# Half-height products from unit 16 on, and weight casts moved to casting transfers, in a convolution with two gated layers

## The chip, the cores and the metric

The kernel runs on one core of a Trainium2 chip. The metric is the device time of one execution in microseconds; the median of three runs of the kernel before is 1130.21 us (1130.08 to 1131.05).

## The reference

Three stages on 2 x 4096 tokens with 192 channels, all in float32:

```python
w = softmax(weight)                       # 8 heads x 7 taps
x = sum over k of w[h, k] * x_pad[s + k]  # causal convolution, 24 channels to a head
h = x @ w_in                              # 192 -> 2048
g = where(h >= 1, h, where(h <= -1, 0, (h + 1)**2 / 4))
x = g @ w_out                             # 2048 -> 192
h = x @ w_in2
out = (h * sigmoid(1.702 * h)) @ w_out2
```

## The kernel before, in words

**Tiles.** The tokens are cut into 16 tiles of 512 (channels on partitions). A layer's 2048 hidden channels are cut into 16 blocks `f` of 128. A *phase* is (layer, token tile); there are 32, and each has 16 *units*, one to a block: 512 units in the order `units`. Units 0 to 31 alternate between the two first phases, four or so at a time (phase 0 has units 0-3, 8-11, 16-19 and 22-25; phase 1 has 4-7, 12-15, 20-21 and 26-31); phase 2 begins with unit 32 and phase 3 with unit 40.

**Precision.** Every float32 operand is split in a high part that TensorE's fp32r format holds and a low part, the difference. A product is hi x hi + hi x lo + lo x hi. 192 channels are 128 + 64 rows: the 64 rows of the high part and the 64 of the low part stand together in a tile `xb`, and swapped (low above) in a tile `xc`, which two SP transfers make from `xb` (`swap_halves`, L184).

**Two forms of the products.** `gemm1` and `gemm2` (L250, L309) work a unit with five products of 128 rows each. `both` (L341) works a *couple*: gemm1 of units u and u + 1 and gemm2 of u - 4 and u - 3, as 38 products of 64 rows in 19 pairs, one in the lower and one in the upper half of the array. In it a unit's gemm1 has nine pieces, because the product lo x lo of the last 64 rows is left out; gemm2 has ten. An even unit reads `xb`, an odd one `xc`. The lower halves of unit u come in pairs 0 to 4, those of unit u + 1 from pair 5 on (its third kind, `xc`, in pair 8), the upper halves of both behind the upper halves of gemm2.

**Two loops.** Up to step `WHOLE` (L511) a step is gemm1 of unit `step`, gemm2 of unit `step - 4`, the activation of the unit (`act_a`: ScalarE twice, then VectorE's max-min L283; `act_b`: ScalarE's cast and VectorE's subtraction, L74 and L75), then what `plan` holds for the step (`beside`). From `WHOLE` on (L525) an iteration is a couple, then `act_a` of both units, `act_b` of both, `beside` of both steps, and last `finish`, which turns a finished phase into the next layer's x tile or into output. The first iteration of this loop still uses gemm1 and gemm2. The order of the program is the order of every engine's queue (`manual_schedule`, L451).

**Weights.** Each tile (layer n, block f) comes as 64-bit words by SP (`weight_load`, L97) and is made into fp32r parts in four pieces (`weight_ops`, L102): begin (ScalarE L118, VectorE's shift L119), join (VectorE L123), high part (a cast, L129, on ScalarE or VectorE), low part (two VectorE subtractions, L133 and L134). `convert_at` (L488) puts these into four consecutive steps from `s` on. For layer 1, f = 8 to 15, `s` is 7, 8, 10, 12, 13, 15, 17, 18; for layer 2, f = 0 to 7, it is 22, 23, 25, 26, 28, 29, 30, 31.

**The start.** SP loads taps, x tiles and the first weight tiles; TensorE does the convolution of a part of the first tiles with diagonal matrices (`conv_on_pe`, L167); the order from L475 on is written by hand. `put_b` (L188) writes `xb` of a layer-1 tile and swaps it only where its phase starts at or behind `WHOLE`. The load of tile (1, 3) is issued by L481, behind that list.

Of the kernel before, what the change touches and what calls it, by code (L numbers as in the profile page):

```python
# [8 lines left out]
F32 = mybir.dt.float32  # L9
F32R = mybir.dt.float32r  # L10
U32 = mybir.dt.uint32
# [4 lines left out]
P = 128  # L16
T = 512
# [3 lines left out]
def kernel(  # L21
# [21 lines left out]
    nc = tc.nc  # L43
    NBLK, D, _ = out.shape
    K = taps_in.shape[2]
    NF, _, WC = w1.shape
    DB = D - P
    B = P // DB
# [1 line left out]
    H = P // 2  # L50
    LAG = 4
    CH = 4
    WHOLE = 2 * NF
    BY_DVE = {(1, f) for f in range(CH, NF, 3)} | {(2, 0), (2, 3)}

    const = ctx.enter_context(tc.tile_pool(name="const", bufs=1))
    wpool = ctx.enter_context(tc.tile_pool(name="wpool", bufs=1))
    stage = ctx.enter_context(tc.tile_pool(name="stage", bufs=2))
# [2 lines left out]
    xs_p = ctx.enter_context(tc.tile_pool(name="xs", bufs=4))  # L61
    a_p = ctx.enter_context(tc.tile_pool(name="a", bufs=3))
    g_p = ctx.enter_context(tc.tile_pool(name="g", bufs=LAG))
    o_p = ctx.enter_context(tc.tile_pool(name="o", bufs=2))
    ps = ctx.enter_context(tc.tile_pool(name="ps", bufs=1, space=bass.MemoryType.PSUM))

    def bank(n, name):
        return ps.tile([P, T], F32, tag=f"bank{n}", name=name)

    def f32(ap):  # L70
        return ap.bitcast(F32)

    def split(src, hi, lo):
        nc.scalar.copy(hi, src)  # L74
        nc.vector.tensor_sub(lo, src, f32(hi))  # L75


    taps = const.tile([P, 2, K], F32, name="taps")
    ident = const.tile([P, P], F32, name="ident")
# [22 lines left out]
    def weight_ops(n, f, s):  # L102

        low, high = s[:, :, 0], s[:, :, 1]  # L110
        w = wt[n][:, f, :]
        m = WC - DB
        st = {}

        def begin():
            a = stage.tile([P, WC], F32, tag="wa", name="wa")
            d = stage.tile([P, WC], U32, tag="wd", name="wd", bufs=3)
            nc.scalar.activation(a, f32(high), AF.Prelu, scale=2.0**-112, alpha=-(2.0**32))  # L118
            nc.vector.tensor_single_scalar(d, low, 29, op=ALU.logical_shift_right)  # L119
            st["a"], st["d"] = a, d  # L120

        def join():
            nc.vector.scalar_tensor_tensor(  # L123
                st["d"], st["a"].bitcast(U32), 3, st["d"], op0=ALU.logical_shift_left, op1=ALU.bitwise_or
            )

        def high_part():
            cast = nc.vector.tensor_copy if (n, f) in BY_DVE else nc.scalar.copy
            cast(w[:, 0:WC], f32(st["d"]))  # L129

        def low_part():
            d = f32(st["d"])
            nc.vector.tensor_sub(w[:, WC + DB : 2 * WC], d[:, 0:m], f32(w[:, 0:m]))  # L133
            nc.vector.tensor_sub(w[:, WC : WC + DB], d[:, m:WC], f32(w[:, m:WC]))  # L134

        return [begin, join, high_part, low_part]


    x1, x2 = {}, {}

    def new_xs():
        return [xs_p.tile([P, T], F32R, tag=t, name=t) for t in ("xah", "xal", "xb", "xc")]
# [21 lines left out]
        for k in range(2):  # L164
            nc.tensor.matmul(w.rearrange("p (k c) -> p k c", c=P), ones, wide, start=k == 0, stop=False)  # L165

    def conv_on_pe(part, t, c, ident, eng_mul, n, fresh):  # L167

        d = o_p.tile([P, K, P], F32, tag="o", name="diag")
        for k in range(n):  # L170
            eng_mul(d[:, k], ident, taps[:, part, k : k + 1])

        def tap(k):
            return lambda: nc.tensor.matmul(c, d[:, k], t[:, k : k + T], start=fresh and k == 0, stop=k == n - 1)  # L174

        return [tap(k) for k in range(n)]

# [6 lines left out]
    def swap_halves(dst, src):  # L184
        nc.sync.dma_start(f32(dst[0:DB]), f32(src[DB:P]))
        nc.sync.dma_start(f32(dst[DB:P]), f32(src[0:DB]))

    def put_b(i, c):  # L188

        b, halved = i % B, phases.index((1, i)) * NF >= WHOLE  # L190
        t = x1[i][2 + (b if halved else 0)]
        hi, lo = (t[0:DB], t[DB:P]) if b == 0 else (t[DB:P], t[0:DB])
        split(c[b * DB : (b + 1) * DB], hi, lo)
        if halved:
            swap_halves(x1[i][3 - b], t)

    def conv_ops(j):

# [19 lines left out]
    phases = [(1, 0), (1, 1), (2, 0), (2, 1), (1, 2)]  # L218
# [4 lines left out]
    def in_turn(*runs):  # L223
        made, us = {}, []
        for p, n in runs:
            f = made.get(p, 0)
            us += [(p, f + k) for k in range(n)]
            made[p] = f + n
        return us

    units = in_turn((0, 4), (1, 4), (0, 4), (1, 4), (0, 4), (1, 2), (0, 4), (1, 6))
# [10 lines left out]
    def hidden_w(u):  # L242
        n, f = phases[units[u][0]][0], units[u][1]
        return wt[n][:, f, 0 : 2 * P], wt[n][:, f, WC + DB : WC + DB + 2 * P]

    def x_of(u):
        n, i = phases[units[u][0]]
        return (x1 if n == 1 else x2)[i]

    def gemm1(u):  # L250

        ah, al, b, _ = x_of(u)
        h = hid[u] = bank(HID + u % 4, f"h{u}")
        hi, lo = hidden_w(u)
        a = [(hi[:, 0:P], ah), (lo[:, 0:P], ah), (hi[:, 0:P], al)]
        bs = [(lo[:, P : 2 * P], b), (hi[:, P : 2 * P], b)]
        prods = a[0::2] + a[1:2] + bs if u < CH else a[0:2] + bs + a[2:]
        for j, (w, r) in enumerate(prods):
            nc.tensor.matmul(h, w, r, start=j == 0, stop=j == len(prods) - 1)  # L259
# [118 lines left out]
    def finish(p, step):  # L378
        n, i = phases[p]
        acc_a, acc_b = accs.pop(p)  # L380
        if n == 1:
            ah, al, b, c = x2[i] = new_xs()
            s = cv_p.tile([P, T], F32, tag="cva", name="s")
            nc.scalar.copy(s[0:DB], acc_b[DB:P])

            def add():
                nc.vector.tensor_add(s[0:DB], acc_b[0:DB], s[0:DB])  # L387

            def put():
                split(s[0:DB], b[0:DB], b[DB:P])  # L390
                if phases.index((2, i)) * NF >= WHOLE:
                    swap_halves(c, b)

            if i < B:
                add()
                split(acc_a, ah, al)
                put()
            else:
                split(acc_a, ah, al)
                at(step + 1, add)  # L400
                at(step + 2, put)
        else:
            o = o_p.tile([P, 2, T], F32, tag="o", name="o")
            nc.scalar.copy(o[0:DB, 1], acc_b[DB:P])
            nc.vector.tensor_add(o[0:DB, 1], acc_b[0:DB], o[0:DB, 1])
            if p < len(phases) - 1:
                nc.scalar.copy(o[:, 0], acc_a)
                nc.sync.dma_start(out[i, 0:P], o[:, 0])
                nc.sync.dma_start(out[i, P:D], o[0:DB, 1])
            else:  # L410
                near, far = slice(0, T // 2), slice(T // 2, T)
                nc.scalar.copy(o[:, 0, near], acc_a[:, near])  # L412
                nc.sync.dma_start(out[i, 0:P, near], o[:, 0, near])
                nc.scalar.copy(o[:, 0, far], acc_a[:, far])  # L414
                nc.scalar.dma_start(out[i, 0:P, far], o[:, 0, far])
                nc.sync.dma_start(out[i, P:D], o[0:DB, 1])


    plan, xt, raw = {}, {}, {}

    def at(step, op):
        plan.setdefault(max(step, 0), []).append(op)
# [4 lines left out]
    def weights_at(n, f):  # L427
        ops = []

        def piece():  # L430
            if (n, f) in raw:
                ops.extend(weight_ops(n, f, raw.pop((n, f))))
            ops.pop(0)()

        return [piece] * 4

    def fetch_x(*which):
        for part, i in which:
# [12 lines left out]
    with tc.manual_schedule():  # L451
# [7 lines left out]
        cb_ps, ca_ps = bank(3, "cb_ps"), bank(2, "ca_ps")  # L459
# [6 lines left out]
            x1[i] = new_xs()  # L466
        ca = cv_p.tile([P, T], F32, tag="cva", name="cva")
        a0 = conv_taps(0, xt[0, 0], ca)
        b_ops = conv_on_pe(1, xt[1, 0], cb_ps, ident, nc.scalar.mul, K, True)
        a1 = conv_on_pe(0, xt[0, 1], ca_ps, ident, nc.gpsimd.tensor_scalar_mul, K - 1, False)  # L470
        for op in b_ops:
            op()

# [14 lines left out]
        def convert_at(n, f, steps):  # L488
            at(steps[0] - 3, lambda: fetch_w(n, f))
            for step, op in zip(steps, weights_at(n, f)):  # L490
                at(step, op)

        for f in range(CH, NF):
            s = f - 2 if f < 2 * CH else 2 * CH - 1 + 5 * (f - 2 * CH) // 3
            convert_at(1, f, range(s, s + 4))
        for f in range(NF):
            s = (22, 23, 25, 26, 28, 29, 30, 31)[f] if f < NF // 2 else 36 + (3 * f - 3 * NF // 2) // 2
            convert_at(2, f, range(s, s + 4))
        for j in range(1, NBLK // B):
            conv_at(j)  # L500

# [8 lines left out]

        for step in range(WHOLE):  # L511
            gemm1(step)
# [6 lines left out]
            if step >= LAG:  # L519
                act_b(step - 1)  # L520
            if step == WHOLE - 1:
                act_b(step)
            beside(step)

        for u in range(WHOLE, len(units) + LAG + 4, 2):  # L525
            v = u - LAG
            if u == WHOLE:
                gemm1(u)
# [70 lines left out]
```

## Time and profile before

| | |
|---|---|
| median of 3 runs | 1130.21 us |
| profiled execution | 1130.99 us, span 1129.2 us |
| TensorE products (PE) | 1124.0 us busy, 9452 |
| TensorE weight loads (PEld) | 921.2 us |
| VectorE (DVE) | 716.0 us, 63% |
| ScalarE (ACT) | 821.2 us, 73% |
| GpSimd (POOL) | 5.9 us, all of it at the start |
| granted clock of TensorE | 1.00 |
| stores of `o`, issue to landing | 2.0 us (256 KB), 2.3 us (128 KB) |

Busy shares are means over the whole span. ScalarE and VectorE are much busier in the first 90 us, in which the weights are made, than later. Idle time of an engine other than the one that ends the chain costs nothing by itself.

### The profile page before, as it was taken

The page shows a single profiled execution, that of the slowest core. Times are in us where ns is not written, and L with a number is a line of the kernel's source. Part 1 is how long each engine was busy: PE and PEld are TensorE (multiplying, and loading weights), DVE is VectorE, ACT ScalarE, POOL GpSimd, SP SyncE. Part 2 cuts the span into 40 slices and gives each one's busy share as a digit, 9 for nine tenths or more (in the row PEclk, how much of TensorE's full clock was granted, in tenths as well). Part 3 has the DMA queues.
Part 4 walks back from the last instruction along what each step waited for, and adds up shares of the span by engine and source line. Part 5 has one row for each costly group of instructions (what it writes and reads, how often), then busy time and mean ns, then how long its engine had stood idle before and what let it go on. Part 6 is the DMA issues. An engine that isn't in the chain of part 4 may idle for free.

```text
span 1129.2 us, 23095 instructions
## 1 busy us (share of the span) xinstructions
PE 1124.0 (100%) x9452; PEld 921.2 (82%) x9452; DVE 716.0 (63%) x1159; ACT 821.2 (73%) x1463; POOL 5.9 (1%) x12
## 2 busy tenths in 40 slices
PE   9999999999999999999999999999999999999998
PEld 5888888888888888888888888888888888888886
DVE  7998867765647656475664756657565575655532
ACT  7998678867768677676876758677586776868654
POOL 2000000000000000000000000000000000000000
PEclk9999999999999999999999999999999999999999
DMA  5434111000010000100010000100001000000000
GB/s 161 140 117 148 34 40 37 11 20 15 11 39 15 20 15 19 40 6 20 15 47 16 2 20 15 49 15 1 20 15 48 16 1 20 15 20 15 11 15 15
DMA packets 16840, 36.68 MB, mean 32 GB/s; under 512 B 2528, under 2 KB 2784, under 8 KB 16736
## 3 DMA queue, kind: packets, MB, share of 16 engines
q1 hardware_dynamic: 16592, 35.09, 10.8%
q8 instruction: 74, 1.21, 0.5%
q14 instruction: 30, 0.25, 0.1%
q10 hardware_dynamic: 144, 0.13, 0.0%
HBM read 21.05 MB, written 6.29 MB: 24 GB/s over the span
## 4 chain that ended last, share of the span: by engine, by line
PE 100%; issue 0%; ACT 0%; DVE 0%
PE acc L370 48%; PE h L370 43%; PE h L259 3%; PE acc L324 3%; PE cb_ps L174 1%; PE ca_ps L174 0%; PE ca_ps L165 0%; ACT o L414 0%; DVE ones L162 0%; ACT o L412 0%
## 5 line engine op out<-in xcount | busy, mean ns | idle before, releaser
L370 PE MATMUL acc<-ghi,wt 64*128 64x512 f32 x2868 | 869.6, 386 | 0.0
L370 PE MATMUL h<-xah,wt 64*128 64x512 f32 x1912 | 738.2, 386 | 0.0
L370 PE MATMUL acc<-glo,wt 64*128 64x512 f32 x1912 | 705.3, 386 | 0.0
L370 PEld LDWEIGHTS acc<-ghi,wt 64*128 64x128 f32 x2868 | 489.5, 184 | 56.3
L75 DVE TENSOR_TENSOR glo<-a,ghi 128x512 fp32r<-128x512 f32 x512 | 341.5, 688 | 231.5 <-ACT ghi L74 221.3
L370 PEld LDWEIGHTS h<-xah,wt 64*128 64x128 f32 x1912 | 351.8, 184 | 37.8 <-issue 0.4
L370 PEld LDWEIGHTS acc<-glo,wt 64*128 64x128 f32 x1912 | 351.8, 184 | 37.8 <-DVE glo L75 0.2
L370 PE MATMUL h<-xal,wt 64*128 64x512 f32 x956 | 369.1, 386 | 0.0
L74 ACT CAST ghi<-a 128x512 fp32r<-128x512 f32 x512 | 301.8, 615 | 28.7 <-DVE a L283 28.5
L283 DVE SCALAR_TENSOR_TENSOR a<-h,a 128x512 f32<-128x512 f32 x256 | 176.6, 690 | 157.6 <-ACT a L282 157.3
L285 ACT ACTIVATE a<-h 128x512 f32<-128x512 f32 x256 | 150.3, 595 | 147.7 <-PE h L370 136.5
L370 PE MATMUL h<-xb,wt 64*128 64x512 f32 x717 | 238.7, 386 | 0.0
L370 PE MATMUL h<-xc,wt 64*128 64x512 f32 x717 | 238.7, 386 | 0.0
L281 ACT ACTIVATE a<-h 128x512 f32<-128x512 f32 x256 | 151.0, 590 | 55.2 <-PE h L370 53.3
L370 PEld LDWEIGHTS h<-xal,wt 64*128 64x128 f32 x956 | 175.9, 184 | 18.7
L282 ACT ACTIVATE a<-a 128x512 f32<-128x512 f32 x256 | 161.9, 632 | 8.2
L370 PEld LDWEIGHTS h<-xc,wt 64*128 64x128 f32 x717 | 131.9, 184 | 17.7
L370 PEld LDWEIGHTS h<-xb,wt 64*128 64x128 f32 x717 | 131.9, 184 | 10.5
L155 DVE SCALAR_TENSOR_TENSOR cva<-xt,taps,cva 128x512 f32<-128x512 f32 x90 | 67.4, 749 | 1.3
L155 DVE SCALAR_TENSOR_TENSOR cvb<-xt,taps,cvb 128x512 f32<-128x512 f32 x42 | 31.3, 746 | 0.5
L74 ACT CAST xb<-s 64x512 fp32r<-64x512 f32 x16 | 9.9, 621 | 29.2 <-DVE s L387 29.2
L324 PE MATMUL acc<-ghi,wt 128*128 128x512 f32 x102 | 29.0, 391 | 0.0
(64 smaller groups left out, 405.1 us busy)
## 6 DMA issues: line engine op xcount, KB each, us to landing
raw<-in_w_dram SPq DMA_DIRECT2D x32, 448.0 KB, 3.4
xc<-xb SPq DMA_DIRECT2D x46, 128.0 KB, 2.3
xt<-in_xa_dram SPq DMA_DIRECT2D x16, 259.0 KB, 2.9
out_dram<-o SPq DMA_DIRECT2D x15, 256.0 KB, 2.0
out_dram<-o SPq DMA_DIRECT2D x17, 128.0 KB, 2.3
xt<-in_xb_dram SPq DMA_DIRECT2D x8, 259.0 KB, 3.1
xb<-xc SPq DMA_DIRECT2D x14, 128.0 KB, 2.2
out_dram<-o ACTq DMA_DIRECT2D x1, 128.0 KB, 1.8
```

Of the source, the lines that this page charges most:

```text
L74: nc.scalar.copy(hi, src)
L75: nc.vector.tensor_sub(lo, src, f32(hi))
L155: return lambda: nc.vector.scalar_tensor_tensor(c, x, w, c, op0=ALU.mult, op1=ALU.add)
L174: return lambda: nc.tensor.matmul(c, d[:, k], t[:, k : k + T], start=fresh and k == 0, stop=k == n - 1)
L259: nc.tensor.matmul(h, w, r, start=j == 0, stop=j == len(prods) - 1)
L281: nc.scalar.activation(a, h, AF.Relu, bias=0.5, scale=0.5)
L282: nc.scalar.activation(a, a, AF.Square)
L283: nc.vector.scalar_tensor_tensor(a, h, 1.0, a, op0=ALU.max, op1=ALU.min)
L285: nc.scalar.activation(a, h, AF.Gelu_apprx_sigmoid)
L324: nc.tensor.matmul(acc, w, r, start=id(acc) in fresh, stop=last and ends[id(acc)] == k)
L370: mm = nc.tensor.matmul(banks[n], w, r, start=n in fresh, stop=ends.get(n) == k)
```

## The change

`WHOLE` falls from 32 to 16: couples begin at unit 16 (in the loop at unit 18). Both x tiles of the first phases are now always swapped, so `put_b` and `finish` always issue the two transfers. The whole form takes `xb` or `xc`, whichever `put_b` wrote.

The high parts of 26 weight tiles, (1, 6) to (1, 15) and (2, 0) to (2, 15), are written by a casting transfer that POOL issues right behind the join; two steps stay empty, and the low part follows three steps behind the join. The pieces of such a tile then take five steps from the same `s`. All other high parts are ScalarE's; VectorE has none.

`wd` has five buffers instead of three, the output tile `o` one instead of two. The diagonal matrices of the second tile's convolution lie in an x buffer.

```diff
-    WHOLE = 2 * NF
-    BY_DVE = {(1, f) for f in range(CH, NF, 3)} | {(2, 0), (2, 3)}
+    WHOLE = NF
+    BY_DMA = {(1, f) for f in range(CH + 2, NF)} | {(2, f) for f in range(NF)}
...
-    o_p = ctx.enter_context(tc.tile_pool(name="o", bufs=2))
+    o_p = ctx.enter_context(tc.tile_pool(name="o", bufs=1))
...
-            d = stage.tile([P, WC], U32, tag="wd", name="wd", bufs=3)
+            d = stage.tile([P, WC], U32, tag="wd", name="wd", bufs=5)
...
         def high_part():
-            cast = nc.vector.tensor_copy if (n, f) in BY_DVE else nc.scalar.copy
-            cast(w[:, 0:WC], f32(st["d"]))
+            if (n, f) in BY_DMA:
+                nc.gpsimd.dma_start(w[:, 0:WC], f32(st["d"]))
+            else:
+                nc.scalar.copy(w[:, 0:WC], f32(st["d"]))
...
-        b, halved = i % B, phases.index((1, i)) * NF >= WHOLE
-        t = x1[i][2 + (b if halved else 0)]
+        b = i % B
+        t = x1[i][2 + b]
...
-        if halved:
-            swap_halves(x1[i][3 - b], t)
+        swap_halves(x1[i][3 - b], t)
...
-        ah, al, b, _ = x_of(u)
+        ah, al, *bc = x_of(u)
+        b = bc[phases[units[u][0]][1] % B]
...
-                if phases.index((2, i)) * NF >= WHOLE:
-                    swap_halves(c, b)
+                swap_halves(c, b)
...
-                ops.extend(weight_ops(n, f, raw.pop((n, f))))
+                begin, join, high, low = weight_ops(n, f, raw.pop((n, f)))
+                if (n, f) in BY_DMA:
+                    wait = lambda: None
+                    ops.extend([begin, lambda: (join(), high()), wait, wait, low])
+                else:
+                    ops.extend([begin, join, high, low])
             ops.pop(0)()
 
-        return [piece] * 4
+        return [piece] * (5 if (n, f) in BY_DMA else 4)
...
-        b_ops = conv_on_pe(1, xt[1, 0], cb_ps, ident, nc.scalar.mul, K, True)
-        a1 = conv_on_pe(0, xt[0, 1], ca_ps, ident, nc.gpsimd.tensor_scalar_mul, K - 1, False)
+        db = o_p.tile([P, K, P], F32, tag="o", name="diag")
+        da = [f32(t).rearrange("p (k c) -> p k c", c=P) for t in new_xs()]
+        b_ops = conv_on_pe(1, xt[1, 0], cb_ps, ident, nc.scalar.mul, [db[:, k] for k in range(K)], True)
+        da = [da[k // 4][:, k % 4] for k in range(K - 1)]
+        a1 = conv_on_pe(0, xt[0, 1], ca_ps, ident, nc.gpsimd.tensor_scalar_mul, da, False)
...
-            convert_at(1, f, range(s, s + 4))
+            convert_at(1, f, range(s, s + 5))
...
-            convert_at(2, f, range(s, s + 4))
+            convert_at(2, f, range(s, s + 5))
```

## Rows read from the trace of the kernel before

**Rows 1.** The page's part 4, the chain that ended last, by engine.
```profile
PE 100%; issue 0%; ACT 0%; DVE 0%
```

**Rows 2.** Windows: the stretch, its length, busy us of each engine, clock, DMA.
```profile
40.00:50.00 10.00, 10.00 (x46) 8.26 (x45) 9.71 (x22) 9.76 (x19) 0.00 (x0) 1.00 0.41 128
```

**Rows 3.** The chain of waits, steps 8 and 9: start us, us, what.
```profile
32.19 1.13 PE acc L324 x5
33.32 1.38 PE h L259 x5
```

**Rows 4.** Timeline, TensorE, first couple: start us, us, engine, line, operation.
```profile
90.43 0.49 PE L370 MATMUL h<-xah,wt 64*128 64x512 f32 x1
```

**Rows 5.** The chain of waits, the tail behind the last couple.
```profile
1120.36 4.79 PE acc L324 x20
```

**Rows 6.** Timeline, TensorE's weight loads that waited, steps 9 and 11.
```profile
33.51 0.19 PEld L259 LDWEIGHTS h<-xah,wt 128*128 128x128 f32 x1 [0.38 <-DVE wt L133]
...
38.26 0.19 PEld L259 LDWEIGHTS h<-xah,wt 128*128 128x128 f32 x1 [0.27 <-DVE wt L133]
```

**Rows 7.** Groups by line and shape, 0 to 140 us: busy us, mean ns | idle.
```profile
L129 ACT CAST wt<-wd 128x448 fp32r<-128x448 f32 x26 | 14.7, 565 | 6.4 <-DVE wd L123 6.2
...
L129 DVE CAST wt<-wd 128x448 fp32r<-128x448 f32 x6 | 2.3, 387 | 0.0
```

**Rows 8.** Timeline, SP's queue: the load of tile (1, 3); swaps and a load.
```profile
8.23 0.33 SPq L99 DMA_DIRECT2D raw<-in_w_dram  x1
...
101.20 0.47 SPq L185 DMA_DIRECT2D xc<-xb  x1
...
102.36 0.59 SPq L99 DMA_DIRECT2D raw<-in_w_dram  x1
```

**Rows 9.** Timeline, the start: low half of xb, begin of tile (1, 3).
```profile
12.89 0.68 DVE L75 TENSOR_TENSOR xb<-cb_ps,xb 64x512 fp32r<-64x512 f32 x1
...
16.76 0.61 ACT L118 ACTIVATE wa<-raw 128x448 f32<-128x448 f32 x1
```

**Rows 10.** The page's part 6, DMA issues: count, KB each, us to landing.
```profile
raw<-in_w_dram SPq DMA_DIRECT2D x32, 448.0 KB, 3.4
xc<-xb SPq DMA_DIRECT2D x46, 128.0 KB, 2.3
```

**Rows 11.** Timeline, VectorE, step 8 and the beginning of step 9.
```profile
36.45 0.69 DVE L283 SCALAR_TENSOR_TENSOR a<-h,a 128x512 f32<-128x512 f32 x1
37.05 0.69 DVE L75 TENSOR_TENSOR glo<-a,ghi 128x512 fp32r<-128x512 f32 x1
37.65 0.56 DVE L133 TENSOR_TENSOR wt<-wd,wt 128x384 fp32r<-128x384 f32 x1
...
38.26 0.62 DVE L123 SCALAR_TENSOR_TENSOR wd<-wa,wd 128x448 uint32<-128x448 uint32 x1
38.79 0.39 DVE L119 TENSOR_SCALAR wd<-raw 128x448 uint32<-128x448 uint32 x1
39.09 0.69 DVE L283 SCALAR_TENSOR_TENSOR a<-h,a 128x512 f32<-128x512 f32 x1
```

**Rows 12.** Timeline, a quiet couple's end on TensorE, then VectorE.
```profile
189.64 0.39 PE L370 MATMUL h<-xah,wt 64*128 64x512 f32 x1
...
190.01 0.69 DVE L283 SCALAR_TENSOR_TENSOR a<-h,a 128x512 f32<-128x512 f32 x1 [1.07 <-ACT a L282]
191.17 0.69 DVE L283 SCALAR_TENSOR_TENSOR a<-h,a 128x512 f32<-128x512 f32 x1 [0.47 <-ACT a L282]
191.78 1.46 DVE L75 TENSOR_TENSOR glo<-a,ghi 128x512 fp32r<-128x512 f32 x2
194.34 0.69 DVE L283 SCALAR_TENSOR_TENSOR a<-h,a 128x512 f32<-128x512 f32 x1 [1.10 <-ACT a L282]
```

**Rows 13.** Timeline, finish of phase 0: copy, and the low half of xb.
```profile
81.74 0.58 ACT L384 COPY s<-acc 64x512 f32<-64x512 f32 x1
...
84.02 0.69 DVE L75 TENSOR_TENSOR xb<-s,xb 64x512 fp32r<-64x512 f32 x1
```

More of the change, by code (lines that the diff above doesn't have):

```diff
@@ L165, in warm_up, with conv_on_pe @@
             nc.tensor.matmul(w.rearrange("p (k c) -> p k c", c=P), ones, wide, start=k == 0, stop=False)
-    def conv_on_pe(part, t, c, ident, eng_mul, n, fresh):
-        d = o_p.tile([P, K, P], F32, tag="o", name="diag")
+    def conv_on_pe(part, t, c, ident, eng_mul, d, fresh):
+        n = len(d)
         for k in range(n):
-            eng_mul(d[:, k], ident, taps[:, part, k : k + 1])
+            eng_mul(d[k], ident, taps[:, part, k : k + 1])
         def tap(k):
-            return lambda: nc.tensor.matmul(c, d[:, k], t[:, k : k + T], start=fresh and k == 0, stop=k == n - 1)
+            return lambda: nc.tensor.matmul(c, d[k], t[:, k : k + T], start=fresh and k == 0, stop=k == n - 1)
         return [tap(k) for k in range(n)]
```

## The prediction

> **What bounds the kernel now.** I read the page's chain of waits first: it is TensorE alone [rows 1], which is busy in 1124.0 of 1129.2 us. So a microsecond of TensorE work removed is a microsecond won, and a wait of TensorE is lost for good. Then the windows: between 40 and 50 us ScalarE is busy 9.76 and VectorE 9.71 of 10 us [rows 2]. There the weights are made beside the activations, and both engines run with almost no room, though TensorE is still last. Third, the price of TensorE's work: five 128-row products take 1.13 us [rows 3], 0.2267 each; from the first couple at 90.43 to the tail at 1120.36 there are 239 couples of 38 products, in 19 pairs, so 1029.93 / 4541 = 0.2268 us for a pair of 64-row products [rows 4, 5]. A pair costs what a whole product costs; only the count differs. Last, TensorE's weight loads: three of them wait for VectorE's low parts (0.38, 0.20, 0.27 us; the first and the last are shown), for the tiles of steps 9, 10 and 11 [rows 6]. These are the only waits on VectorE's weights in the trace, and they show that the low parts come just in time there.
>
> **The gain.** A unit's first product takes five whole products, in halves nine pieces, that is 4.5 pairs. Before, units 0 to 33 are whole (32 and 33 open the second loop), after it 0 to 17. 16 units x 0.5 x 0.2268 = **-1.81 us**. The second product costs five slots either way.
>
> **ScalarE and VectorE.** 26 high parts leave them: 20 on ScalarE net of tile (1,4), which moves to it (0.565 us each), 6 on VectorE (0.387) [rows 7]. Neither ends the chain, so this is worth nothing by itself; it counts only where a wait below gets shorter.
>
> **The start.** The 64-row form needs both layouts of the first two x tiles, so put_b now issues a swap for them. The swap of tile 0 stands on SP's queue ahead of the load of weight tile (1,3), which was issued at 8.23 [rows 8]. It waits for the low half of xb, done at 12.89 + 0.68 = 13.57 [rows 9]; two swap issues occupy SP for 102.36 - 101.20 = 1.16 us before the next load [rows 8]; landing takes 3.4 [rows 10]. So the tile is there at about 18.15, and ScalarE, which took it up at 16.76 [rows 9], stands until then: 1.4 us. The load of (1,6) is queued behind the second swap the same way, but its tile is wanted only at some 28 us.
> Next, the low parts of (1,6) and (1,7) are written a step later than before. VectorE's order in step 8 is: max-min, low part of the activation, low part of (1,7), join, begin, then step 9's max-min at 39.09 [rows 11]. Moved to step 9, behind that and another subtraction (0.60 each), the low part of (1,7) starts at 39.09 + 1.20 = 40.29 and its first piece ends 0.55 later, against a load at 38.26 [rows 6]: 2.6 us. Two casts of 0.30 that VectorE loses pull the other way (2.0); the 1.4 us of the late tile push (4.0). Following the queues step by step I get a low part at 41.04, a load at 41.64: **+3.4 us**, bounds 2.0 and 4.0. The smaller waits before it (step 3, steps 8 to 10) are contained in it.
>
> **The couples.** Before, a low part of step s reaches TensorE four steps later. Now the weight steps of a couple are written behind both activations, and the next couple starts at once. A quiet couple shows the time table: couple ends at 189.64, VectorE's two max-min start 0.37 and 1.53 later, its two subtractions end 191.78 + 1.46 = 193.24, 3.60 after the couple's end, and the next max-min comes at 194.34 [rows 12]. From issue to issue a subtraction takes 0.60, a low part 0.61 (0.55 to the end of its first piece), a join 0.53, a begin 0.30 [rows 11]; weight work has 1.16 us a couple before it makes the next one late.
> - Tile (1,11): low part in step 16, used by unit 19, sixth pair of the couple (18, 19). The products of unit 17 end one block (1.13) before that couple begins, so the subtractions end 3.60 - 1.13 = 2.47 after its start, the low part at 2.94, the load at 3.0. It is due at 5 x 0.2268 - 0.23 = 0.90, and 0.13 late costs nothing (a load waited 0.38 where the products slipped 1.38 - 1.13 = 0.25 [rows 3, 6]): **+2.0 us**.
> - Tile (1,15): low part in step 22, used by unit 25 in the very next couple (24, 25), sixth pair. Low part at 3.52 + 0.55 = 4.07, load at 4.12, due at 1.03: 3.0; tile (1,14), written in step 21 by a VectorE 0.8 us late, adds 0.1 at the couple's first pair: **+3.1 us**.
> - The first x tile of the second layer. finish of phase 0 now comes behind the couple (28, 29) and its weight steps, and couple (32, 33), one couple later (4.31), reads it in both layouts. Couple 26 leaves VectorE late: two lows, two joins, a begin = 2.59 against 1.16, so 1.4. Then two max-min, two subtractions, begin, low, join, begin, add, two subtractions: the low half of x ends 8.15 after couple (28, 29). Before it went from the copy at 81.74 to 84.71 [rows 13] with three steps to spare. The swap lands 2.3 later [rows 10], at 10.4; pair 9 of couple (32, 33) is due at 4.31 + 8 x 0.2268 - 0.10 = 6.0: **+4.4 us**, with no lateness 3.6. Some 1.6 of it shows at the couple's first pair (xah), 1.4 at the second (xal), 1.4 at the swap.
>
> The bounds of these three: 1.0 to 2.5, 2.0 to 4.0, 2.5 to 5.5; they fall if VectorE reaches the low part earlier than in the quiet couple, and rise if it comes late.
>
> **The casting transfers.** The trace has none. SP's swaps of 128 KB land after 2.3 us, the weight loads of 448 KB after 3.4 [rows 10]; the new ones move 224 KB, and POOL, which issues them, has nothing else after the start. I take 4 us. From join to low part VectorE has 5.2 us of other work for (1,6), 4.0 for (1,14), 4.3 for (2,2), more elsewhere, so at 4 us they are hidden and cost 0. The Trainium skill ("SBUF — State Buffer", "Who interferes with whom") has a rule against this: GpSimd writes the descriptors through a port that VectorE's fast copies and casts lock. One such form stays, the 0.39 us shift of each tile [rows 11]; by the page it delays a transfer by no more than that. "DMA: Bandwidth & Descriptors" gives 2.0 us plus bytes at 436 GB/s, an estimate of 2.5 us; no run here shows either.
>
> **At nothing.** One output tile instead of two: outputs follow each other 16 units or more apart (8 once, some 17 us), and a store lands after some 2 us. The diagonals in an x buffer and five wd buffers: no tile is asked for before its last reader is done.
>
> **Sum.** 3.4 + 2.0 + 3.1 + 4.4 - 1.8 = +11.1. The profiled execution took 1130.99 (span 1129.2 and 1.8 around it), so 1142.1; it lies 0.78 above the median of 1130.21, so **1141.3 us**.
>
> **Rivals.**
> - *The transfers outlast their cover*: VectorE then stands at the low part with all activations queued behind it, and TensorE waits for them. It decides from 4.0 us. At 8 us: 2.8 at step 10, about 3.0 at couple 24, 3.7 at couple 32: 1150.8. For it: 128 rows of 1792 B with a conversion, issued in software. Against: 4 us is already more than the larger loads take.
> - *The low parts are in time, only the x tile is late*: -1.8 - 0.5 (the three old slips) + 4.4 = 1132.3. For it: 11.3 us less work on ScalarE. Against: the order of the queue, not its load, puts the low part of (1,15) behind the activations of the couple just ended.
> - *No wait at all* (the other side): VectorE, without its casts and with ScalarE early, writes every low part and x before its pair. -1.81 - 0.48 = 1127.9. It decides where VectorE reaches the low part of (1,15) 3 us earlier than in the quiet couple. Against: that is before the products of unit 23 have left TensorE.
> - *It does not do what it says*: switching earlier changes neither count nor waits: 1130.2. For it only that the 16 units are 3% of the work.
> A fall of TensorE's granted clock in the new waits is not priced: in every window of before it is 1.00, and no wait was this long. It belongs to the upper end.
>
> **How the numbers follow.** Forecast (1134 to 1147) 0.62, late transfers 0.14, x tile alone 0.12, no wait 0.07, nothing 0.05. The range 1131.5 to 1151.5 leaves out no wait, nothing, a part of x alone and of late transfers, about 0.2. A measurement here tells 0.2%, 2.26 us. Faster: no wait, 0.06 of its 0.07, as it lies on the limit. Same: the rest of it, nothing, and 0.04 of x alone, 0.10. Slower: 0.84.
>
> **What would show it.** Right: the load of (1,3) issued near 14.8 us; weight loads of TensorE waiting for low parts in steps 8 to 11, in the sixth pair of couples (18, 19) and (24, 25); in couple (32, 33) waits for xah, xal and the swap; a steady couple of 4.31 afterwards. Wrong: no waits behind step 12, or VectorE waiting for POOL's transfers.

## The result: 15.8 us slower, 5 us more than forecast

The changed kernel takes 1146.39 us, median of four (1145.50 to 1149.99); the kernel before, run beside it, 1130.56 us. The ratio is 1.0148, 95% interval 1.0135 to 1.0160. The forecast was 1141.3 us, slower, 1134 to 1147 as the likely part of a range of 1131.5 to 1151.5; the time lies inside, near the upper end of that part.

The profiled execution is the longest of the four: 1149.99 us with a mean granted clock of 0.994; the others have 0.997 (1145.50 and 1145.94) and 0.995 (1146.84). So the trace shows more loss than the median. The line numbers shown here are two higher than before from L135 on (the low part is L135 and L136).

The page after, parts 1 and 4, and two rows of part 6:

```profile
PE 1130.1 (98%) x9596; PEld 1021.2 (89%) x9596; DVE 716.2 (62%) x1153; ACT 814.7 (71%) x1443; POOL 20.0 (2%) x38
...
PE 94%; DVE 2%; DMA 2%; ACT 2%; issue 0%; SPq 0%; ACTq 0%
...
raw<-in_w_dram SPq DMA_DIRECT2D x32, 448.0 KB, 4.0
...
wt<-wd POOLq DMA_DIRECT2D x26, 224.0 KB, 4.0
```

The change does what it says: 144 products more than the 9452 of before, 16 units with 4 pieces more in gemm1 and 5 in gemm2. But the chain, TensorE alone before [rows 1], now has 6% of other engines. Its last step, the tail behind the last couple:

```profile
1138.72 4.79 PE acc L326 x20
```

Before it began at 1120.36 [rows 5], so 18.36 us must lie ahead of it. (The two profiled executions differ by 19.0 us. The other 0.6 lies behind: from the start of the tail to the end of the span it is 9.5 us, before 8.8.) TensorE's weight loads with their waits say where (start us, us, engine, line, operation, [idle before <- what ended it]):

```profile
39.22 0.19 PEld L261 LDWEIGHTS h<-xah,wt 128*128 128x128 f32 x1 [1.66 <-DMA wt<-wd]
39.81 0.19 PEld L261 LDWEIGHTS h<-xah,wt 128*128 128x128 f32 x1 [0.41 <-DVE wt L135]
...
42.45 0.19 PEld L261 LDWEIGHTS h<-xah,wt 128*128 128x128 f32 x1 [0.50 <-DVE wt L135]
...
58.32 0.18 PEld L372 LDWEIGHTS h<-xah,wt 64*128 64x128 f32 x1 [0.35 <-DVE a L285]
...
61.23 0.18 PEld L372 LDWEIGHTS h<-xah,wt 64*128 64x128 f32 x1 [1.92 <-DVE wt L135]
...
73.94 0.18 PEld L372 LDWEIGHTS h<-xah,wt 64*128 64x128 f32 x1 [1.00 <-DVE wt L135]
...
77.31 0.28 PEld L372 LDWEIGHTS h<-xah,wt 64*128 64x128 f32 x1 [2.37 <-DVE wt L135]
...
98.06 0.18 PEld L372 LDWEIGHTS h<-xah,wt 64*128 64x128 f32 x1 [1.96 <-ACT xah L74]
...
101.18 0.28 PEld L372 LDWEIGHTS h<-xal,wt 64*128 64x128 f32 x1 [2.93 <-DVE xal L75]
...
105.00 0.28 PEld L372 LDWEIGHTS h<-xc,wt 64*128 64x128 f32 x1 [1.19 <-DMA xc<-xb]
```

Read it by differences of start times, against 0.2268 us a pair and 4.31 us a couple:

- Step 11's load is at 42.45, before at 38.26 [rows 6]: **+4.2** (gemm1 of unit 12 shows the same, 44.63 against 40.47).
- Couple (18, 19), first to sixth pair: 2.91 for 5 x 0.2268 = 1.13: **+1.8**.
- From there to the first pair of couple (24, 25): 12.71 for 14 pairs and two couples, 11.79: **+0.9**. To its sixth pair: 3.37 for 1.13: **+2.2**.
- From there to couple (32, 33): 20.75 for 14 pairs and three couples, 16.10: **+4.65**. Only 1.96 of it is the wait for xah; the rest is the next view.
- First to second pair of couple (32, 33): 3.12 for 0.23: **+2.9** (xal). From there to couple (34, 35), which starts at 108.67: 7.49 for 4.08: **+3.4** (swap, and again the next view).
- Another 0.1 is lost behind that, and the halves give back 1.8 (16 units of half a pair, as forecast). The sum is 18.4, the shift of the tail.

The missing view is the clock. Windows of the same kernel (stretch, its length, busy us of PE, PEld, DVE, ACT, POOL, clock, DMA share and GB/s):

```profile
76.00:78.00 2.00, 0.69 (x4) 0.60 (x6) 1.81 (x6) 1.08 (x3) 0.00 (x0) 0.64 0.00 0
78.00:80.00 2.00, 2.00 (x12) 1.54 (x10) 0.72 (x2) 0.00 (x0) 0.53 (x1) 0.50 0.60 159
80.00:82.00 2.00, 2.00 (x12) 1.57 (x10) 0.00 (x0) 0.44 (x1) 0.00 (x0) 0.50 0.95 327
82.00:84.00 2.00, 2.00 (x14) 1.54 (x14) 0.69 (x1) 1.13 (x3) 0.00 (x0) 0.65 0.30 95
84.00:86.00 2.00, 2.00 (x22) 1.76 (x20) 1.04 (x2) 1.72 (x4) 0.00 (x0) 1.00 0.00 0
...
102.00:104.00 2.00, 2.00 (x12) 1.44 (x10) 1.18 (x2) 1.96 (x4) 0.00 (x0) 0.50 0.43 102
```

After the two waits of couple (24, 25), TensorE is busy without a gap, and yet a window of 2 us counts 12 products instead of 22: granted 0.50, which is 1.2 instead of 2.4 GHz. The timeline shows a pair every 0.427 us (78.33, 78.75, 79.18), where the quiet stretch has 0.2268. The Trainium skill ("TensorE: Matmul & The Clock Gate", section "Wait — 56ns, not 53.3ns?") gives 426.7 ns for 512 columns at the lower level, and the trace agrees. The same comes back behind the xal wait.

Three smaller readings. SP's queue (start, us): the load of (1, 3), 8.23 before [rows 8], now stands behind both swaps, as forecast for 14.8.

```profile
13.60 0.54 SPq L187 DMA_DIRECT2D xc<-xb  x1
14.26 0.51 SPq L188 DMA_DIRECT2D xc<-xb  x1
14.87 1.49 SPq L99 DMA_DIRECT2D raw<-in_w_dram  x3
```

The chain of waits, two transfers on it (start, us from issue to landing):

```profile
33.92 5.25 DMA wt<-wd
...
92.79 5.59 DMA wt<-wd
```

And VectorE's low part behind the second of them, on its timeline:

```profile
98.41 0.56 DVE L135 TENSOR_TENSOR wt<-wd,wt 128x384 fp32r<-128x384 f32 x1 [1.58 <-DMA wt<-wd]
```

The 26 transfers land after 2.1 to 5.9 us, median 4.0. VectorE waits for five of them, 4.2 us in all, and the xal of couple (32, 33) is queued behind this one.

### The profile page after: what moved, and what is told of

It reads as the page before. It is cut to its first block, busy times and chain, and to the rows that moved or that the text cites. A ratio compares the mean times of both kernels' runs of the same rounds, so it can differ in the third digit from the quotient of the medians.

```text
span 1148.2 us, 23428 instructions
## 1 busy us (share of the span) xinstructions
PE 1130.1 (98%) x9596; PEld 1021.2 (89%) x9596; DVE 716.2 (62%) x1153; ACT 814.7 (71%) x1443; POOL 20.0 (2%) x38
## 3 DMA queue, kind: packets, MB, share of 16 engines
q1 hardware_dynamic: 16912, 35.61, 11.1%
## 4 chain that ended last, share of the span: by engine, by line
PE 94%; DVE 2%; DMA 2%; ACT 2%; issue 0%; SPq 0%; ACTq 0%
PE acc L372 49%; PE h L372 43%; PE acc L326 1%; DMA wt<-wd 1%; PE h L261 1%; ACT a L284 0%; DVE a L285 0%; DVE glo L75 0%; DVE wt L135 0%; ACT a L283 0%; DMA raw<-in_w_dram 0%; ACT ghi L74 0%; DMA xc<-xb 0%; DVE wd L123 0%; ACT wa L118 0%
## 5 line engine op out<-in xcount | busy, mean ns | idle before, releaser
L372 PE MATMUL acc<-ghi,wt 64*128 64x512 f32 x2964 | 907.9, 388 | 0.0
L372 PE MATMUL h<-xah,wt 64*128 64x512 f32 x1976 | 766.0, 388 | 5.5 <-DVE wt L135 4.0
L372 PE MATMUL acc<-glo,wt 64*128 64x512 f32 x1976 | 737.4, 388 | 0.0
L372 PEld LDWEIGHTS acc<-ghi,wt 64*128 64x128 f32 x2964 | 513.5, 185 | 27.1
L372 PEld LDWEIGHTS h<-xah,wt 64*128 64x128 f32 x1976 | 365.3, 185 | 25.6 <-DVE wt L135 5.3
L372 PE MATMUL h<-xal,wt 64*128 64x512 f32 x988 | 383.1, 388 | 2.6 <-DVE xal L75 2.6
L372 PEld LDWEIGHTS acc<-glo,wt 64*128 64x128 f32 x1976 | 365.3, 185 | 18.6 <-DVE glo L75 0.2
L372 PE MATMUL h<-xc,wt 64*128 64x512 f32 x741 | 247.8, 388 | 0.5 <-DMA xc<-xb 0.5
L372 PE MATMUL h<-xb,wt 64*128 64x512 f32 x741 | 247.4, 387 | 0.0
L118 ACT ACTIVATE wa<-raw 128x448 f32<-128x448 f32 x32 | 19.1, 610 | 5.5 <-DMA raw<-in_w_dram 4.1
```

Of the source, the lines that this page charges most:

```text
L372: mm = nc.tensor.matmul(banks[n], w, r, start=n in fresh, stop=ends.get(n) == k)
```

## The experiments

Each is the changed kernel with the edit shown, unless said otherwise.

**Transfers taken out, couples kept** (couples_only): casts on ScalarE and VectorE as before, in four steps.

```diff
-    BY_DMA = {(1, f) for f in range(CH + 2, NF)} | {(2, f) for f in range(NF)}
+    BY_DMA = set()
+    BY_DVE = {(1, f) for f in range(CH, NF, 3)} | {(2, 0), (2, 3)}
...
+            cast = nc.vector.tensor_copy if (n, f) in BY_DVE else nc.scalar.copy
+            cast(w[:, 0:WC], f32(st["d"]))
```

> The changed kernel with the casts back on ScalarE and VectorE as in the kernel before (four steps for a tile, low part one step earlier); couples still begin at unit 16. Theory (the waits come from the order of the queues: late low parts, late x tile, a weight load behind a swap, and the clock falls in the longest waits): start about +1.5, no wait in couple (18, 19), about 0.3 in couple (24, 25), about 4 in couple (32, 33) with 0 to 3 of clock, gain -1.8: 1134 to 1138. Rival (the loss is the transfers' own lateness): no loss left, 1128 to 1131.

Measured 1144.34 us (1143.58 to 1145.11), ratio 1.0123: 6 to 10 us above the theory, and further above the rival. TensorE's loads from couple (24, 25) on (lines are one higher than before there):

```profile
71.25 0.18 PEld L371 LDWEIGHTS h<-xah,wt 64*128 64x128 f32 x1 [2.83 <-DVE wt L134]
...
93.61 0.18 PEld L371 LDWEIGHTS h<-xah,wt 64*128 64x128 f32 x1 [4.60 <-ACT xah L75]
...
95.97 0.28 PEld L371 LDWEIGHTS h<-xal,wt 64*128 64x128 f32 x1 [2.17 <-DVE xal L76]
...
99.65 0.29 PEld L371 LDWEIGHTS h<-xc,wt 64*128 64x128 f32 x1 [1.05 <-DMA xc<-xb]
```

Couple (18, 19) no longer waits. Couple (24, 25) waits 2.83 us at its first pair, where 0.3 was expected, and the waits for the first x tile of layer 2 are longer than with the transfers (4.60, 2.17, 1.05 us against 1.96, 2.93, 1.19). That ScalarE and VectorE then also carry the casts is the likely reason; no run isolates it. Most of the loss comes with the couples at unit 16, whoever casts.

The clock in the two stretches (columns as above): it stays at 1.00 behind the wait of 2.83 us and falls behind the waits of couple (32, 33).

```profile
70.00:80.00 10.00, 8.75 (x76) 7.23 (x78) 8.81 (x18) 8.23 (x15) 0.00 (x0) 1.00 0.30 93
...
90.00:100.00 10.00, 4.21 (x18) 2.68 (x20) 8.81 (x18) 7.61 (x14) 0.00 (x0) 0.73 0.29 79
```

**Couples taken out, transfers kept** (transfers_only):

```diff
-    WHOLE = NF
+    WHOLE = 2 * NF
```

> The changed kernel with couples from unit 32 as before; transfers, three steps and both swaps stay. Theory: the start's +4.2 alone, granted clock 1.00, no wait behind step 12: 1134 to 1135.5. Rival (transfers late wherever they are): VectorE stands for them in steps 20 to 36 too and the time stays above 1139.

Measured 1135.34 us (1135.19 to 1137.89), ratio 1.0043: the time is as expected. The trace has the start's waits alone (1.62, 0.44, 0.93, 0.47, 1.98, 0.41 us) and none behind. The clock of 1.00 that was expected did not hold in the profiled execution, the longest of the four (1137.89 us, the others 1135.19 to 1135.38): behind the wait for a transfer at the start it is 0.50 from 42 to 45 us.

```profile
40.09 0.19 PEld L261 LDWEIGHTS h<-xah,wt 128*128 128x128 f32 x1 [1.98 <-DMA wt<-wd]
```

```profile
40.00:50.00 10.00, 9.82 (x35) 7.68 (x36) 8.28 (x18) 6.73 (x13) 1.24 (x3) 0.83 0.57 172
```

The two parts, some 14 and 5 us, add up to more than the 15.8 of the change: both contain waits at the start, and with the transfers the x tile's waits are shorter.

**The casts at the same place, by ScalarE** (scalar_casts):

```diff
-            if (n, f) in BY_DMA:
-                nc.gpsimd.dma_start(w[:, 0:WC], f32(st["d"]))
-            else:
-                nc.scalar.copy(w[:, 0:WC], f32(st["d"]))
+            nc.scalar.copy(w[:, 0:WC], f32(st["d"]))
```

> The changed kernel with the 26 transfers replaced by ScalarE casts at the same place of the program; the low parts stay three steps behind the join. Theory: only what transfers took beyond their cover goes (1.7 at step 10, 0.6 in couple 24, 1.6 in couple 28), ScalarE gets 12 us more; the queue order keeps the rest with the clock's fall: 1141 to 1145. Rival (late transfers): most of the loss goes, below 1136.

Measured 1177.44 us, ratio 1.0416, clock 0.984: a miss of 32 us. ScalarE's waits between 20 and 130 us (engine, line, what it waited for: us, times, longest):

```profile
ACT wt L128 <- DVE wd L123: 26.1, 16, 2.0
```

The cast stands right behind the join in program order, so ScalarE stops until VectorE has come to it, 16 times, with the next activations queued behind. So the run doesn't compare the cost of a cast by the two ways, as it was meant to; the fall of the clock and ScalarE's own casts are in the 32 us too. It shows what POOL gives: in the changed kernel POOL stands 105 us for VectorE's `wd` in the first 130 us, and no activation is queued behind it.

**The clock: waits filled** (filled_waits): 39 products with discarded results in the waits of couples (18, 19), (24, 25) and (32, 33).

```diff
+    FILL = {(18, 10): 8, (24, 0): 3, (24, 10): 9, (32, 0): 7, (32, 2): 12}
...
+            for _ in range(FILL.get((u, k), 0)):
+                nc.tensor.matmul(banks[HID + (u + 1) % 4], wt[1][:, 0, 0:P], x1[1][0], start=True, stop=True)
```

> The changed kernel with 39 extra products, whose results are overwritten, put into TensorE's waits of couples 18, 24 and 32 (8, 3, 9, 7, 12 of 0.227 us, about as long as each wait). Theory (TensorE's standing still makes the granted clock fall): granted clock 1.00 in every window, pairs at 0.227 us behind the waits, and 3.4 to 6 us less: 1140.5 to 1143.5. Rival (the clock falls for another reason): clock 0.994 to 0.997 as before and no gain, 1146 or more.

Measured 1145.97 us (1145.88 to 1147.27), ratio 1.0140; clock 0.999, and 1.00 in every window of 10 us from 20 to 130. Of the theory the clock held and the time did not: the fillers ran past their waits. Couple (24, 25), the fillers and its sixth pair:

```profile
76.02 1.92 PEld L374 LDWEIGHTS h<-xah,wt 128*128 128x128 f32 x9 [0.37 <-issue]
78.29 0.18 PEld L375 LDWEIGHTS h<-xah,wt 64*128 64x128 f32 x1 [0.35 <-DVE wd L119]
```

The sixth pair stands at 78.29 (77.31 without fillers) and waits for no low part any more. The next run has shorter ones.

**Shorter fillers** (short_fill): 22 products, with the same loop.

```diff
+    FILL = {(18, 10): 5, (24, 10): 6, (32, 0): 4, (32, 2): 7}
```

> As filled_waits, but with 22 extra products (results discarded) instead of 39: 5 in the wait of couple 18, 6 in that of couple 24, 4 and 7 in those of couple 32, each shorter than its wait. Theory (standing still makes the clock fall; the first fillers gave the gain back because they ran 2 us past what they waited for): clock 0.998 or more, the waits behind the fillers short, 1142 to 1144 us, 2.5 to 4.5 below the changed kernel. Rival (the clock costs less than the profiled execution shows, or falls in the shorter waits as well): 1145.5 to 1147 us.

Measured 1144.83 us (1144.47 to 1146.07), ratio 1.0129; clock 0.999. The time lies between the two expectations. By the medians only 1.6 us are won, and the 95% intervals of the two ratios overlap (1.0116 to 1.0143, 1.0135 to 1.0160); by the profiled executions 5.3 are won (the tail begins at 1133.38). The loads behind the fillers in couple (32, 33):

```profile
94.49 0.18 PEld L375 LDWEIGHTS h<-xah,wt 64*128 64x128 f32 x1 [0.82 <-ACT xah L74]
...
97.58 0.18 PEld L375 LDWEIGHTS h<-xal,wt 64*128 64x128 f32 x1 [1.21 <-DVE xal L75]
...
100.56 0.18 PEld L375 LDWEIGHTS h<-xc,wt 64*128 64x128 f32 x1 [1.51 <-DMA xc<-xb]
```

Here the waits are seen at full clock. The sixth pair of couple (24, 25) is at 76.55: 17.94 to xah for 16.10, 3.09 to xal for 0.23, 2.98 to xc for seven pairs, 1.59: 1.8 + 2.9 + 1.4 = 6.1 us for the x tile. The changed kernel loses 4.65 + 2.9 + 3.4 = 10.95 over the same stretch, so 4.9 of it go with the clock. Not all of that is additional: a TensorE at half speed comes later to the swap and waits less for it (1.19 us, here 1.51).

**The load of (1, 3) ahead of the first swap** (load_first):

```diff
-        order += a0[0:5] + ws[0][0:1] + [lambda: first_tap(0, xt[0, 1], ca_ps, K - 1)] + ws[0][1:3]
+        order += a0[0:5] + ws[0][0:1] + [lambda: fetch_w(1, 3)] + [lambda: first_tap(0, xt[0, 1], ca_ps, K - 1)] + ws[0][1:3]
...
-        fetch_w(1, 3)
```

> The changed kernel with the load of weight tile (1, 3) issued right behind the begin of tile (1, 0), ahead of the first swap on SP's queue. Theory: of the start's 4.2 us the part of the late tile goes, 1.4 to 2; the low parts of (1, 6) and (1, 7) stay a step late: 1144 to 1145.5. Rival (the start's loss is the transfer of (1, 6) alone): no change, 1146.4.

Measured 1145.47 us (1145.02 to 1145.82), ratio 1.0135: at the upper end of what was expected. The waits of step 3 (1.77 and 0.44) are gone and step 11's load is at 40.16 instead of 42.45, so the late tile was worth 2.3 us at that point of the trace. The median moved 0.9, which is not clear of the spread (the changed kernel's executions lie up to 4.5 us apart). The clock was 0.996 here.

**Layer 1's weights earlier** (early_weights):

```diff
-            s = f - 2 if f < 2 * CH else 2 * CH - 1 + 5 * (f - 2 * CH) // 3
+            s = f - 2 if f < 2 * CH else (7, 8, 10, 11, 12, 13, 15, 16)[f - 2 * CH]
```

> The changed kernel with the weight steps of layer 1, blocks 11 to 15, one or two steps earlier (s = 11, 12, 13, 15, 16 instead of 12, 13, 15, 17, 18). Theory: the waits of couples (18, 19) and (24, 25) go, 1.9 + 2.8, and the fall of the clock behind the second, 2.9: about 7.6 less, 1137.5 to 1140. Rival (ScalarE and VectorE are full there, the wait only moves): less than 2 us.

Measured 1140.61 us (1139.86 to 1144.00), ratio 1.0098: a little above the theory, 5.8 below the changed kernel. The waits of couples (18, 19) and (24, 25) are gone; behind step 11 only the x tile's stay (2.24, 2.09, 0.75 us).

**finish of phase 0 ahead of the activations** (finish_first):

```diff
+            if v < len(units) and units[v + 1] == (0, NF - 1):
+                finish_if_last(v + 1, u + 1)
             if u < len(units):
                 for op in (act_a, act_b):
...
-            finish_if_last(v + 1, u + 1)
+            if units[min(v + 1, len(units) - 1)] != (0, NF - 1):
+                finish_if_last(v + 1, u + 1)
```

> The changed kernel with the finish of phase 0 right behind its couple, ahead of the activations and weight steps of that couple. Theory: the three waits of couple (32, 33), 5.0 us, and the fall of the clock in them, 2.9, go, less up to 1 where the activations of units 28 and 29 come late: 1138.5 to 1141. Rival (VectorE's load decides, not the order): less than 2 us.

Measured 1145.32 us (1143.67 to 1145.69), ratio 1.0131: the theory missed; 1.1 us less is the rival's time. The waits for x are gone, and these stand in their place:

```profile
95.45 0.18 PEld L372 LDWEIGHTS h<-xah,wt 64*128 64x128 f32 x1 [1.00 <-DVE a L285]
...
96.38 0.18 PEld L372 LDWEIGHTS acc<-ghi,wt 64*128 64x128 f32 x1 [0.75 <-ACT ghi L74]
...
97.20 0.18 PEld L372 LDWEIGHTS acc<-glo,wt 64*128 64x128 f32 x1 [0.52 <-DVE glo L75]
...
107.80 0.18 PEld L372 LDWEIGHTS h<-xah,wt 64*128 64x128 f32 x1 [1.60 <-ACT a L287]
```

What goes first on VectorE makes what comes second late: the max-min of units 28 and 29 has to empty the bank that couple (32, 33) writes. The waits of couple (24, 25) (1.05 and 2.33 us) and the clock's fall behind them are still there, as nothing was changed ahead of them.

**All three together** (mended): load_first, early_weights and finish_first, and the high parts of (1, 6) and (1, 7) by ScalarE in four steps.

> All three orders mended at once (load first, early weight steps, finish first), and tiles (1, 6) and (1, 7) cast by ScalarE in four steps, so 24 transfers; couples from unit 16. Theory: all waits of step 8 and later gone, the gain of 1.8 left, clock 1.00: 1128 to 1130. Rival (ScalarE and VectorE can't keep up with couples while the weights are made): 1132 or more.

Measured 1135.50 us (1135.05 to 1136.93), ratio 1.0048: 5.5 to 7.5 us above the theory, the rival's time. Couple (32, 33) again waits for the max-min (1.60), ghi (0.75) and glo (0.52), and behind these three the clock falls, though none is as long as 2 us:

```profile
85.68 0.18 PEld L372 LDWEIGHTS h<-xah,wt 64*128 64x128 f32 x1 [1.60 <-DVE a L285]
```

```profile
85.00:90.00 5.00, 3.81 (x19) 2.46 (x21) 4.46 (x10) 4.69 (x9) 0.12 (x1) 0.82 0.54 136
```

**A couple more for the x tile** (phase_early): phase 0 ends one couple earlier, finish at its old place, layer 1's weights closer together; the load of (1, 3) and the casts of (1, 6) and (1, 7) as in mended.

```diff
-    units = in_turn((0, 4), (1, 4), (0, 4), (1, 4), (0, 4), (1, 2), (0, 4), (1, 6))
+    units = in_turn((0, 4), (1, 4), (0, 4), (1, 4), (0, 8), (1, 8))
...
+            s = f - 2 if f < 2 * CH else (7, 8, 10, 11, 12, 13, 14, 15)[f - 2 * CH]
...
+            s = (18, 20, 21, 22, 28, 29, 30, 31)[f] if f < NF // 2 else 36 + (3 * f - 3 * NF // 2) // 2
```

> Phase 0 gets units 16 to 23 and phase 1 units 24 to 31, so that the first x tile of the second layer is finished behind couple (26, 27), one couple earlier; the weights of layer 1 are made at s = 7, 8, 10, 11, 12, 13, 14, 15, the first four of layer 2 at 18, 20, 21, 22; the load of (1,3) is ahead of the swap and (1,6), (1,7) are cast by ScalarE in four steps. Theory (the loss is the order of work in the queues of VectorE and ScalarE; where x and each weight tile have a couple more, nothing waits): only 1 to 1.5 us of waits in steps 7 to 11 stay, the clock stays at 1.00, 1128.5 to 1130.5 us. Rival (VectorE and ScalarE have no capacity for a tile in each of the steps 11 to 15): low parts late at units 12 to 16 and in couples 18 to 22, with waits of 1 us and more: 1132 to 1136 us.

Measured 1134.32 us (1134.02 to 1135.28), ratio 1.0037: the rival's time, and its wait in couple (20, 21). The others are of the kind of those in mended, for the max-min, ghi and glo behind a finish; the longest are shown.

```profile
58.74 0.18 PEld L372 LDWEIGHTS h<-xah,wt 64*128 64x128 f32 x1 [0.99 <-DVE wt L135]
...
85.02 0.18 PEld L372 LDWEIGHTS h<-xah,wt 64*128 64x128 f32 x1 [0.49 <-DVE a L285]
...
96.77 0.18 PEld L372 LDWEIGHTS h<-xah,wt 64*128 64x128 f32 x1 [1.49 <-ACT a L287]
```

VectorE is busy 9.96 of 10 us from 40 to 50 and 9.65 in the next 10; no wait is over 1.5 us, and the clock is 1.00 in every window of 10 us from 20 to 110.

**More room everywhere** (room_for_all): as phase_early, with couples from unit 22 (`WHOLE = NF + 4`), wider steps for layer 2 (17, 18, 20, 22, 23, 24, 28, 29), and

```diff
-            if i < B:
+            if i == 0:
                 add()
-                split(acc_a, ah, al)
                 put()
+                plan.setdefault(step + 1, []).insert(0, lambda: split(acc_a, ah, al))
```

> As phase_early, but couples from unit 22 on (in halves 12 units fewer than before instead of 16, a gain of 12 x 0.1134 = 1.36 us), the first four weight tiles of layer 2 spread wider (s = 17, 18, 20, 22, 23, 24, 28, 29), and the first x tile of layer 2 made in two iterations: copy, add, xb and swap behind couple (26, 27), xah and xal behind the activations of couple (28, 29); the second x tile as the later ones are. Theory (waits come from the order and from too little room in one couple; with this room none is left but 1 to 1.5 us in steps 7 to 11): 1128.9 to 1130.5 us, clock 1.00. Rival (work taken from one couple makes the next one late, VectorE being nearly full from 30 to 100 us): again 2 to 4 us of waits in couples 24 to 36, 1132 to 1134.5 us.

Measured 1138.73 us (1137.49 to 1139.54), ratio 1.0071: the rival's kind of loss, and 4 us more than it. The x tile again, now xah, which the edit put behind the activations of couple (28, 29):

```profile
88.52 0.28 PEld L372 LDWEIGHTS h<-xah,wt 64*128 64x128 f32 x1 [3.44 <-ACT xah L74]
```

**One wait by itself** (single_wait): the kernel before, with one max-min done ten times, far behind the weights.

```diff
+            for _ in range(10 if u == 212 else 1):
-            nc.vector.scalar_tensor_tensor(a, h, 1.0, a, op0=ALU.max, op1=ALU.min)
+                nc.vector.scalar_tensor_tensor(a, h, 1.0, a, op0=ALU.max, op1=ALU.min)
```

> The kernel before, with one max-min of VectorE (unit 212, far behind the weights) done ten times instead of once; the result is the same. 9 x 0.60 = 5.4 us of VectorE work make TensorE wait about 2 to 3 us, once, in couple (216, 217). Theory (the clock falls in such a wait and comes back only some us later, which was the term left out of the sum): the tail comes 4.5 to 6 us later, of which the wait 2 to 3 and the pairs behind it at half clock 2 to 3; 1134.5 to 1136.5 us. Rival (the clock of the changed kernel falls for another reason, such as the many waits together): only the wait, 1132 to 1133.5 us, clock 1.00 in every window.

Measured 1137.18 us (1136.11 to 1139.67), ratio 1.0065: above both expectations. The wait, and windows around it:

```profile
485.79 0.18 PEld L371 LDWEIGHTS h<-xah,wt 64*128 64x128 f32 x1 [4.20 <-DVE a L284]
```

```profile
480.00:482.00 2.00, 2.00 (x18) 1.59 (x14) 1.93 (x3) 0.00 (x0) 0.00 (x0) 1.00 0.00 0
482.00:484.00 2.00, 0.01 (x1) 0.00 (x0) 1.90 (x4) 0.00 (x0) 0.00 (x0) 1.00 0.00 0
484.00:486.00 2.00, 0.21 (x1) 0.18 (x1) 1.93 (x4) 0.23 (x1) 0.00 (x0) 1.00 0.00 0
486.00:488.00 2.00, 1.98 (x9) 1.24 (x10) 1.62 (x3) 1.97 (x4) 0.00 (x0) 0.50 0.00 0
488.00:490.00 2.00, 2.00 (x16) 1.59 (x14) 1.37 (x3) 1.76 (x4) 0.00 (x0) 0.65 0.00 0
490.00:492.00 2.00, 2.00 (x20) 1.69 (x18) 1.30 (x3) 1.26 (x3) 0.00 (x0) 1.00 0.00 0
```

In a trace whose clock is 1.00 everywhere else, one wait halves it. The pair due at 481.85 starts at 485.79, 3.9 us late (2 to 3 expected). Behind it another 1.2 us (2 to 3 expected) go to short waits for ghi and glo and to pairs at half clock: from 487.03 to 489.16 one starts every 0.427 us. The tail begins 5.15 us later than before, in the shortest of the five executions. That a wait alone can make the clock fall is shown.

## Why the prediction was right in kind and 5 us short

The sum of the prediction, put beside what the traces show (changed kernel; couple (32, 33) at full clock from short_fill):

| term | predicted | measured |
|---|---|---|
| start, to step 11 | +3.4 | +4.2 |
| couple (18, 19) | +2.0 | +1.8 |
| couple (24, 25), both pairs | +3.1 | +3.2 |
| first x tile: xah, xal, swap | +4.4 (1.6, 1.4, 1.4) | +6.1 (1.8, 2.9, 1.4) |
| gain of the halves | -1.8 | -1.8 (by count; the sum of starts above closes with it to 0.1) |
| sum without clock | +11.1 | +13.4 |
| clock | not priced | +5.0 in the profiled execution, about 1.8 of the median's 15.8 |
| behind the tail | not priced | +0.6 |

- *Right*: the place of every wait, the kind of nearly all, and that the gain, half a pair for each of 16 units, is small against them. The signs that the prediction named are all there: the load at 14.87, the low parts of steps 8 to 11, the sixth pairs, xah, xal and the swap, and a couple every 4.31 us afterwards. So is one of its two signs of being wrong: VectorE waits for POOL's transfers. (For the sixth pair of couple (24, 25) the sum takes 3.0 where its own terms give 4.12 - 1.03 = 3.09.)
- *What failed* are two steps, of about the same weight in the median. One is "A fall of TensorE's granted clock in the new waits is not priced". Waits of 2 to 3 us were on the list, and before had none that long, so its clock of 1.00 said nothing about them. Such waits can have a second price, here about 2.8 and 2.0 us behind couples (24, 25) and (32, 33) (the changed kernel against short_fill), and at most 1.2 in single_wait. filled_waits and single_wait show that it comes with the waits. It does not come with each: in couples_only the clock stays at 1.00 behind a wait of 2.83 us, while in mended it falls behind three of 1.60, 0.75 and 0.52. What decides between them stays open. The 1.8 us of the median are a remainder (15.8 - 13.4 - 0.6), not a measurement; short_fill won 1.6.
- The other is *the transfers*, "at 4 us they are hidden and cost 0", some 2.3 us: the median is 4.0, but single ones take 5.25 and 5.59. The first puts 0.8 on the start: TensorE itself waits for the high part of (1, 6), 1.66 us. The second keeps VectorE 1.58 us ahead of xal, and xal is 1.5 later than forecast. A third, of (1, 14), moves loss within couple (24, 25): 0.9 to its first pair (0.1 forecast), where VectorE waits 0.59 us for it, and 2.2 to the sixth (3.0). The prediction had given 4.0 us as the point from which this decides, and took just that value for all 26. The Trainium skill ("DMA: Bandwidth & Descriptors", section "Anatomy of one DMA") makes it 2.5 us, an estimate from its fixed cost and rate; the measured 4.0 decides.
- *Lateness of transfers as the main cause*, the first rival, is out: couples_only loses 1.2%, some 14 us, without them. A part of it came true all the same, the 2.3 us above.
- *No wait at all*, the rival on the other side, was not reached by any of the versions that move work about. In phase_early, the best with couples, the tail begins at 1122.60, 2.24 behind the kernel before, though its halves save 1.8. Some 0.8 us of its loss lie elsewhere: 0.3 between the tail and the end of the span, 0.5 between the span and the measured time (2.3 us, before 1.8). In the kernels with 26 transfers 0.6 to 0.7 lie behind the tail, in couples_only and scalar_casts, which have none, 0.1. That goes with the transfers; why, no run shows.

No version beats the kernel before. The nearest are transfers_only (1135.3), mended (1135.5) and phase_early (1134.3), each 0.4 to 0.5% slower, with a 95% interval wholly above 1. What stays open is whether some order without any wait exists; from 30 to 60 us VectorE is over 9.6 of 10 us busy in the best one.

## What to carry to other kernels

When a change saves a fraction of a microsecond per step on the bound engine and moves the work that feeds it, follow the feeding engine's queue instruction by instruction: in the prediction that gave the waits to within 0.2 us, save where a transfer was late. It did less well for the rearranged versions, where couples_only, finish_first, mended and room_for_all each had waits that were not on the list. Put a fall of the clock into the range of a forecast that has new waits of one to three us: here it fell behind some of them and not behind others. Price transfers by their slow ones too, since the consumer stands in a queue and one late landing delays all behind it. Moving work in a nearly full queue is worth something where there is room ahead (early_weights won 5.8 us, phase_early 12.1); where there is none it chooses what will be late, as in finish_first.

## What the runs showed of the hardware that was not expected

- A wait of 2.9 us (xal) and a pair of waits of 1.0 and 2.4 us within 4 us were followed by a granted clock of 0.50 for some 5 us, and 3.9 us in single_wait by 0.50 and 0.65 for some 3 us; behind the pair of waits TensorE was busy without a gap in all of that time.
- The length of one wait does not settle whether the clock falls. It stayed at 1.00 behind 2.83 us in couples_only and behind 1.92 us in the changed kernel (couple (18, 19)). It fell behind 1.98 and 0.41 us in transfers_only and behind 1.60, 0.75 and 0.52 us in mended.
- How often it falls differs from one execution to the next of the same kernel, and the time with it: early_weights took 1140.6 us at a clock of 0.997 and 1144.0 at 0.993.
- 26 casting transfers of 224 KB from SBUF to SBUF took 2.1 to 5.9 us, median 4.0, while swaps of 128 KB took 2.2.
